# Delta-rule attention with a gated MLP: small products with 32-column stationaries in place of masked 64-column blocks

## The chip, the cores and the metric

The kernel runs on one core of one Trainium2 chip. The metric is device time in microseconds (us), from launch to the last output; lower is better. TensorE (PE) does the matrix products, its weight loads are shown as PEld; VectorE (DVE), ScalarE (ACT) and GpSimd (POOL) do elementwise work; SyncE (SP) issues most DMAs. A matmul loads a *stationary* operand (rows x columns) into the array and streams a *moving* operand through it.

## The reference

32 sequences (4 batches x 8 heads) of 768 tokens with head dimension 48 run a delta rule. All heads of a token are then joined to 384 channels, which pass through a gated MLP with 2048 hidden units.

```python
k_n = k / (np.linalg.norm(k, axis=-1, keepdims=True) + 1e-06)
for t in range(S):
    y[:, :, t] = np.einsum('bhd,bhde->bhe', q[:, :, t], state)
    v_old = np.einsum('bhde,bhd->bhe', state, kt)
    state = state + bt[:, :, :, None] * np.einsum('bhd,bhe->bhde', kt, vt - v_old)
...
h = x @ w_in
g = h - np.tanh(h)
return (g @ w_out).astype(np.float32)
```

## The kernel before, in words

**Tiling.** Time is cut into 24 chunks of 32 tokens (`C = 32`, `NS = 24`). A chunk holds 32 (batch, head) pairs of 32 x 32 (scores) or 32 x 48 (values). With 4 batches on the partitions, one chunk fills 128 partitions by 8 heads. Four chunks are a group (`NG = 6`), and four chunks are also one window of 512 tokens of the MLP (`W = 4`, six windows).

**One chunk.** `score` makes the key-key and key-query products. `solve(g)` inverts the 32 x 32 triangular systems of a whole group on DVE, a chain of some 60 dependent elementwise instructions that starts with a transpose (line 356) once all four chunks of the group are scored, and ends with another (line 438), which writes `tt`. `chain` then runs through the chunks one by one, since each needs the state that the one before left: keys times state (line 552), queries times state (570), subtraction from the values (`vsub`, 560), the inverted block times these (585), a copy to SBUF (`u_sb`, 591), two products that update the state (603), two by two additions into `st` (631), and the product of masked scores with the chunk values (614). `output` copies, transposes on PE (650) and splits the result into a high and a low part for the MLP.

**How two batches share a product.** A product covers two batches at a time. The stationary operand is a block matrix of 64 columns: keys or queries of two batches side by side (`kb`, `qb`, 112 rows, zero off the blocks), the inverted block doubled and masked (`tb`, lines 506), the scores doubled and masked (`pc`, 514). These blocks are built by copies: ACT copies keys and queries (lines 304 to 313, 526, 531), POOL builds `tb` and `pc` (DVE does it for the first four chunks), and ACT moves the scores out of PSUM (`pq`, 341).

**MLP.** For each window and each of 16 slices of 128 hidden units, nine matmuls with 512 moving columns make the hidden values (`ph`, line 722), `gate` works on them on ACT and DVE (733 to 742), and nine more accumulate the output (`po`, 765). Window 0 is done in two halves of 256 tokens. The weights arrive as 64-bit numbers in 32 pieces and are decoded on ACT and DVE (671 to 697) while window 0 runs.

**What sets the order.** `Plan` writes the order of every engine by hand, in advance: each step is an `Op` with an engine, an assumed cost, what it depends on and a rank. `run` picks the engine that can start first, and on it, among the steps that can start within `SLACK` (2.2 us on PE) of the earliest, the one with the smallest start less rank. Each engine then executes its list strictly in that order. PSUM has two banks `psa` for all small products, one `psy`, two `ph` and three `po`. `Ring` counts free buffers. Until a set time (46 us in the plan) PE's gaps are filled with dummy matmuls (`warm`, line 220).

## Time and profile before

| | us |
|---|---|
| median of 3 runs | 685.51 (680.96 to 686.44) |
| span of the profiled execution | 683.6 |
| PE busy | 634.8 |
| DVE busy | 424.5 |
| ACT busy | 294.6 |
| POOL busy | 77.9 |
| first MLP matmul starts | 69.4 |
| the second group's inverted blocks reach PE | 178.4 |
| first MLP matmul of window 1 starts | 220.4 |

The profiled execution's own time is known by its span, from the first to the last instruction; the runs' times take in the little that lies around it as well. Each fp32 product is executed as two passes, so 16 products stand as x32 in the rows. PE is busy for most of the span, but busy at two speeds: the row PEclk of the page gives the granted clock in tenths. Rows of a timeline give start, length, engine, line, operation, output and inputs, shape, count, and in brackets how long the engine had been idle and what ended that.

### The profile page before, as it was taken

The page shows a single profiled execution, that of the slowest core. Times are in us where ns is not written, and L with a number is a line of the kernel's source. Part 1 is how long each engine was busy: PE and PEld are TensorE (multiplying, and loading weights), DVE is VectorE, ACT ScalarE, POOL GpSimd, SP SyncE. Part 2 cuts the span into 40 slices and gives each one's busy share as a digit, 9 for nine tenths or more (in the row PEclk, how much of TensorE's full clock was granted, in tenths as well). Part 3 has the DMA queues.
Part 4 walks back from the last instruction along what each step waited for, and adds up shares of the span by engine and source line. Part 5 has one row for each costly group of instructions (what it writes and reads, how often), then busy time and mean ns, then how long its engine had stood idle before and what let it go on. Part 6 is the DMA issues. An engine that isn't in the chain of part 4 may idle for free.

```text
span 683.6 us, 18248 instructions
## 1 busy us (share of the span) xinstructions
PE 634.8 (93%) x7922; PEld 545.0 (80%) x7922; DVE 424.5 (62%) x982; ACT 294.6 (43%) x560; POOL 77.9 (11%) x81
## 2 busy tenths in 40 slices
PE   7697999899597998999989998999999999999996
PEld 4386999889596887888888887888878888888885
DVE  6975685898436884689737886388862434243242
ACT  4454369743354335642465235652342333233232
POOL 1000000100412004300133003310061000000000
PEclk9857589999558999999999999999999999999999
DMA  9439903000343004410153102430000010001001
GB/s 255 167 116 344 272 19 114 19 1 36 105 117 104 0 1 133 129 54 15 59 160 88 40 0 68 129 110 1 0 25 26 2 46 1 0 1 47 0 1 46
DMA packets 25056, 48.80 MB, mean 71 GB/s; under 512 B 3168, under 2 KB 15584, under 8 KB 24976
## 3 DMA queue, kind: packets, MB, share of 16 engines
q1 hardware_dynamic: 24832, 47.49, 22.9%
q8 instruction: 62, 1.02, 0.7%
q10 hardware_dynamic: 144, 0.15, 0.1%
q14 instruction: 18, 0.15, 0.1%
HBM read 42.91 MB, written 4.72 MB: 70 GB/s over the span
## 4 chain that ended last, share of the span: by engine, by line
PE 75%; issue 10%; ACT 6%; DVE 6%; DMA 2%; POOL 1%; SPq 0%; ACTq 0%; POOLq 0%; DVEq 0%
PE po L765 26%; PE ph L722 25%; PE psa L603 7%; PE psy L614 4%; PE psa L585 3%; PE psa L326 3%; PE psa L552 3%; PE psy L570 2%; ACT qb L531 1%; ACT kb L526 1%; PE psa L650 1%; DMA kd<-in_kq 1%; DVE st L631 1%; ACT u_sb L591 1%; ACT kb L313 1%
## 5 line engine op out<-in xcount | busy, mean ns | idle before, releaser
L722 PE MATMUL ph<-xt,w 128*128 128x512 f32 (+1 forms) x1008 | 211.8, 365 | 3.3 <-DVE t L735 2.7
L765 PE MATMUL po<-gh,w 128*128 128x512 f32 (+1 forms) x1008 | 211.8, 363 | 1.8 <-ACT gh L740 0.6
L722 PEld LDWEIGHTS ph<-xt,w 128*128 128x128 f32 x1008 | 173.8, 193 | 33.2 <-DVE t L735 3.7
L765 PEld LDWEIGHTS po<-gh,w 128*128 128x128 f32 x1008 | 171.2, 190 | 31.8 <-ACT gh L740 1.3
L733 ACT ACTIVATE t<-ph 128x512 f32<-128x512 f32 (+1 forms) x112 | 60.1, 537 | 153.9 <-PE ph L722 145.2
L735 DVE TENSOR_TENSOR t<-ph,t 128x512 f32<-128x512 f32 (+1 forms) x112 | 68.8, 615 | 80.1 <-ACT t L733 79.3
L740 ACT CAST gh<-t 128x512 fp32r<-128x512 f32 (+1 forms) x112 | 62.7, 559 | 86.2 <-PE po L765 40.8
L742 DVE TENSOR_TENSOR gh<-t,gh 128x512 fp32r<-128x512 f32 (+1 forms) x112 | 71.8, 642 | 43.6 <-ACT gh L740 41.5
L631 DVE TENSOR_TENSOR st<-st,psa 48x384 f32<-48x384 f32 x88 | 48.6, 552 | 62.9 <-PE psa L603 61.5
L603 PE MATMUL psa<-u_sb,kt 32*48 32x48 f32 x1472 | 49.2, 223 | 8.7 <-ACT u_sb L591 7.3
L603 PEld LDWEIGHTS psa<-u_sb,kt 32*48 32x48 f32 x1472 | 43.0, 136 | 15.1 <-ACT u_sb L591 9.7
L428 DVE TENSOR_TENSOR a<-a,tmp 128x30 f32<-128x30 f32 (+9 forms) x150 | 49.5, 330 | 4.1
L424 DVE TENSOR_TENSOR tmp<-a 128x30 f32<-128x30 f32 (+9 forms) x150 | 49.6, 331 | 3.7
L506 POOL TENSOR_TENSOR tb<-tt,cs 128x512 f32<-128x512 f32 x20 | 25.5, 1274 | 201.4 <-DVE tt L438 161.1
L585 PE MATMUL psa<-v,tb 64*64 64x48 f32 x768 | 31.6, 236 | 13.5 <-POOL tb L506 9.1
L585 PEld LDWEIGHTS psa<-v,tb 64*64 64x64 f32 x768 | 28.4, 150 | 15.6 <-POOL tb L506 9.3
L614 PE MATMUL psy<-u_sb,pc 64*64 64x48 f32 x768 | 31.9, 239 | 3.0 <-issue 2.2
L552 PEld LDWEIGHTS psa<-st,kb 112*64 112x64 f32 x736 | 27.3, 156 | 6.6 <-issue 3.1
L614 PEld LDWEIGHTS psy<-u_sb,pc 64*64 64x64 f32 x768 | 28.6, 153 | 4.8 <-issue 3.4
L552 PE MATMUL psa<-st,kb 112*64 112x48 f32 x736 | 29.6, 240 | 2.6 <-DVE st L631 2.4
L526 ACT COPY kb<-kd 48x512 f32<-48x512 f32 x44 | 27.1, 616 | 9.2 <-PE psa L552 8.7
L326 PE MATMUL psa<-kc,kb 112*64 112x64 f32 x704 | 29.8, 246 | 0.5 <-issue 0.3
(85 smaller groups left out, 521.6 us busy)
## 6 DMA issues: line engine op xcount, KB each, us to landing
kc<-in_kq SPq DMA_DIRECT2D x23, 448.0 KB, 4.1
kd<-in_kq SPq DMA_DIRECT2D x22, 448.0 KB, 4.0
raw<-in_w_in SPq DMA_DIRECT2D x16, 384.0 KB, 8.7
raw<-in_w_out SPq DMA_DIRECT2D x16, 384.0 KB, 8.2
v<-in_vn SPq DMA_DIRECT2D x24, 192.0 KB, 4.3
kt<-in_kn SPq DMA_DIRECT2D x24, 192.0 KB, 2.9
out<-o SPq DMA_DIRECT2D x18, 256.0 KB, 2.0
cs<-in_const ACTq DMA_DIRECT2D x1, 144.5 KB, 4.6
```

Of the source, the lines that this page charges most:

```text
L326: nc.tensor.matmul(ps[64 * pr:64 * pr + 64, h, :], cols(kb, u), kc[:, :, u, :], start=True, stop=True)
L552: nc.tensor.matmul(pk[64 * pr:64 * pr + 64, h, :], cols(kb, u), st[:, pr, h, :], start=True, stop=True)
L585: nc.tensor.matmul(pu[rows, h, :], tb[rows, h].rearrange("p b i -> p (b i)"), v[rows, h, :], start=True, stop=True)
L603: nc.tensor.matmul(ps[HALF[bp], h, :], kt[rows, h, :], u_sb[rows, h, :], start=True, stop=True)
L614: nc.tensor.matmul(py[rows, h, :], pc[rows, h].rearrange("p b i -> p (b i)"), u_sb[rows, h, :], start=(s == 0), stop=True, skip_group_chec ...
L631: nc.vector.tensor_tensor(st[rows, pr], st[rows, pr], ps[rows], ALU.add)
L722: nc.tensor.matmul(p, wi[f][:, a, ct, :], xt[:, b, ct, part], start=(ct == 0 and i == 0), stop=(ct == NC - 1 and i == 2))
L733: nc.scalar.activation(t_, p, AF.Tanh)
L735: nc.vector.tensor_tensor(t_, p, t_, ALU.subtract)
L740: nc.scalar.copy(gh[:, 0, :n], t_)
L742: nc.vector.tensor_tensor(gh[:, 1, :n], t_, gh[:, 0, :n].bitcast(F32), ALU.subtract)
L765: nc.tensor.matmul(po[c][:, part], wo[f][:, a, 128 * c:128 * c + 128], gh[:, b, :n], start=(f == 0 and i == 0 and z < 1), stop=(f == NF - ...
```

## The change

Each batch gets a product of its own, with a 32-column stationary, so that no block matrices have to be built. Where a block structure is still needed it moves to the *moving* operand, which may be wide.

- **Scores** (`products`): 32 products of 48 rows x 32 columns straight from the loaded keys, in place of 16 of 112 x 64 from copied ones. The first four chunks do keys first and queries later (`answers`), and load keys and queries as separate halves.
- **Masks**: DVE masks the scores as it takes them out of PSUM (`mask`, 256 elements). ACT's `pq` copy and POOL's `tb` and `pc` are gone, and so are all key and query copies with the tiles `kb` and `qb`.
- **Chain**: keys and queries times state are 16 products each with the loaded `kd` (112 x 32) and a block-diagonal state of 96 columns. The inverted block is used as it is, 32 products of 32 x 32. ACT spreads the chunk values with two scaled copies into a block-diagonal `ub`. The state update takes 16 products of 64 x 48 with 96 moving columns, in place of 32 of 32 x 48. The last product takes 32 of 32 x 32.
- **Loads**: a second host layout, `kp`, serves the scores and `kq` the chain; every chunk loads both.
- **Plan**: the order of chunk work changes. A PE step may carry a `hold` in place of the slack; chain steps after the first group hold PE for at most 0.2 us. Queries times state now stand after the inverted block, and the output product in a stream of its own. The dummy matmuls are issued in any gap until the first output unit of the MLP. Pool sizes change (`SOLS` 3 to 4, nine `pc`).

```diff
+    def products(ps, kc, x):
+        for u in range(16):
+            h, pr = divmod(u, 2)
+            for bp, rows in enumerate(HALF):
+                q = slice(64 * pr + 32 * bp, 64 * pr + 32 * bp + 32)
+                nc.tensor.matmul(ps[q, h, :], kc[rows, 0, u, :], kc[rows, x, u, :], start=True, stop=True)
+
+    def mask(s, ps, psr, scored):
+        (_, t) = yield Op("DVE", dve(256), (scored, const_in, rpc), 0.3)
+        pc = at.tile([128, H, C], F32, name="pc", bufs=PCS)
+        nc.vector.tensor_tensor(pc, ps[:, :, C:], strict, ALU.mult)
...
-            for bp, rows in enumerate(HALF):
-                nc.scalar.copy(kb[rows, :, bp, :], kc[rows, 0])
...
-        for u in range(16):
-            h, pr = divmod(u, 2)
-            nc.tensor.matmul(ps[64 * pr:64 * pr + 64, h, :], cols(kb, u), kc[:, :, u, :], start=True, stop=True)
...
-        hw.tensor_tensor(tb, tt[:, 8 * r:8 * r + 8, None, :].broadcast_to([128, H, 2, C]), blocks, ALU.mult)
...
-        hw.tensor_tensor(pc, pq[:, :, None, :].broadcast_to([128, H, 2, C]), strict, ALU.mult)
...
-            nc.scalar.copy(kb[rows, :, bp, :], kd[rows, 0])
...
-            nc.scalar.copy(qb[rows, :, bp, :], kd[rows, 1])
...
                 for u in range(16):
-                    h, pr = divmod(u, 2)
-                    nc.tensor.matmul(pk[64 * pr:64 * pr + 64, h, :], cols(kb, u), st[:, pr, h, :], start=True, stop=True)
...
+                    m, b = divmod(u, 4)
+                    nc.tensor.matmul(pk[32 * b:32 * b + 32, 2 * m:2 * m + 2, :], kd[:, 0, 4 * b + m, :], st[:, b, m],
+                                     start=True, stop=True)
...
+            for u in range(32):
+                h, b = divmod(u, 4)
+                rows = slice(32 * b, 32 * b + 32)
+                nc.tensor.matmul(pu[rows, h, :], tt[rows, 8 * r + h, :], v[rows, h, :], start=True, stop=True)
...
+                nc.scalar.activation(ub[:, :, 0], pu, AF.Copy, scale=odd[0])
...
+                nc.scalar.activation(ub[:, :, 1], pu, AF.Copy, scale=odd[1])
...
+                        nc.tensor.matmul(ps[HALF[h % 2], h // 2], kt[rows, h, :], ub[rows, h], start=True, stop=True)
...
+            nc.tensor.matmul(py[rows, h, :], pc[rows, h, :], ub[rows, h, b % 2, :],
+                             start=(s == 0), stop=True, skip_group_check=True)
...
+CHAIN_RANK, CHAIN_HOLD = 2.5, 0.2
...
-EXTRA = {0: ["v0"], 1: ["d1"], 3: ["v1"], 9: ["v2"], 13: ["k4"], 18: ["v3"], 24: ["b1"]}
+EXTRA = {0: ["q0"], 1: ["v0", "q1"], 2: ["q2", "d1"], 3: ["q3", "v1"], 7: ["d2"], 9: ["v2"], 13: ["k4"], 15: ["d3"], 18: ["v3"], 24: ["b1"]}
```

The order of the instructions shows what moved. On PE, in the third group of chunks, one chunk's steps stood close together before (`psa` and `psy` are PSUM tiles, `kb`/`qb` key and query blocks, `st` the state, `v` the values, `tb` and `pc` masked blocks, `u_sb` the chunk values, `kt` keys by token):

```order
L326 MATMUL psa<-kc_3539,kb_85 64x64 x16
L552 MATMUL psa<-st,kb_84 64x48 x16
L570 MATMUL psy<-st,qb_87 64x48 x16
L585 MATMUL psa<-v,tb 64x48 x16
L650 MATMUL psa<-cs,y_sb 128x128 x3
L603 MATMUL psa<-u_sb,kt 48x48 x16
L614 MATMUL psy<-u_sb,pc 64x48 x16
L603 MATMUL psa<-u_sb,kt 48x48 x16
```

Now, at the same place (`ub` are the spread chunk values; L746 and L701 are the MLP's output and hidden units):

```order
L303 MATMUL psa<-kc_3896 32x64 x32
L522 MATMUL psa<-st,kd_3493 32x96 x16
L746 MATMUL po_3626<-gh,w_1742 128x512 x3
L746 MATMUL po_3627<-gh,w_1742 128x512 x3
L746 MATMUL po_3628<-gh,w_1742 128x512 x3
L543 MATMUL psa<-v,tt_3835 32x48 x32
L565 MATMUL psy<-st,kd_3493 32x96 x16
L303 MATMUL psa<-kc_4003 32x64 x32
L629 MATMUL psa<-cs,y_sb 128x128 x3
L701 MATMUL ph<-xt_3177,w_1640 128x512 x9
L575 MATMUL psa<-ub,kt 48x96 x16
L593 MATMUL psy<-ub,pc 32x48 x32
```

An MLP unit now stands in each gap of a chunk's chain, also in the first chunks of a group, and the small products are 32 wide.

On ACT, while window 0 runs and the second group is scored (`gs` takes the key products, `t` and `gh` belong to the gate, `c` and `w` to the decoding of weights), these rows stood before:

```order
L313 COPY kb_85<-kc_1133 48x16x32 x2
L733 ACTIVATE t<-ph 128x256 x2
L740 CAST gh<-t 128x256 x2
L337 COPY gs_1229<-psa 128x8x32
L341 COPY pq<-psa 128x256
L733 ACTIVATE t<-ph 128x256
L526 COPY kb_83<-kd_1155 48x16x32 x2
L740 CAST gh<-t 128x256
L531 COPY qb_86<-kd_1155 48x16x32 x2
L733 ACTIVATE t<-ph 128x256
L526 COPY kb_84<-kd_1162 48x16x32 x2
L740 CAST gh<-t 128x256
```

And now:

```order
L347 COPY gs_1301<-psa 128x8x32
L674 CAST w_1853<-c_1768 128x384
L650 ACTIVATE c_1949<-raw_1442 128x384
L347 COPY gs_1301<-psa 128x8x32
L674 CAST w_1948<-c_1801 128x384
L712 ACTIVATE t<-ph 128x256
L650 ACTIVATE c_1985<-raw_1445 128x384
L719 CAST gh<-t 128x256
L712 ACTIVATE t<-ph 128x256
L674 CAST w_1967<-c_1834 128x384
L347 COPY gs_1301<-psa 128x8x32
```

The key copies are out of the row, and the second and third copies of `gs` stand closer together.

On SP, the first loads were these before:

```order
L227 DMA kc_94<-in_kq 112x1024
L227 DMA kc_100<-in_kq 112x1024
L227 DMA kd_103<-in_kq 112x1024
L227 DMA kd_109<-in_kq 112x1024
L246 DMA bt<-in_beta 128x32
L258 DMA raw_118<-in_w_in 128x3x256
```

And now:

```order
L230 DMA kc_91<-in_kp 112x512
L230 DMA kc_95<-in_kp 112x512
L230 DMA kd_99<-in_kp 112x512
L230 DMA kd_102<-in_kp 112x512
L249 DMA bt<-in_beta 128x32
L261 DMA raw_106<-in_w_in 128x3x256
L230 DMA kc_91<-in_kp 112x512
```

The first four key loads are half as large, and the query halves follow among the weights.

More of the change, by code (lines that the diff above doesn't have):

```diff
@@ L618, in chain @@
-            if s + 1 < NS:
-                state[s] = added[1]
-    def add(s, pr, ps, psr, e, added):
-        for n, rows in enumerate(HALF):
-            if s == 0 and pr:
-                (_, t) = yield Op("ACT", act(DM, True), (e, zero[5]), 2.5)
-                nc.scalar.copy(st[rows, pr], ps[rows])
-            else:
-                (_, t) = yield Op("DVE", dve(DM), (e, zero[5]), 1.5)
+                    m, b = divmod(u, 4)
+                    nc.tensor.matmul(py[32 * b:32 * b + 32, 2 * m:2 * m + 2, :], kd[:, 1, 4 * b + m, :], st[:, b, m],
+                                     start=(m == 0), stop=False, skip_group_check=True)
@@ L759, in out_units @@
             if w not in pos:
+                if not pos:
+                    plan.streams[:] = [x for x in plan.streams if x[0] is not idle]
                 pos[w] = ([ps_o.tile([128, T], F32, name=f"po{c}") for c in range(NC)], ro.take())
@@ L810, in preps @@
             yield from prep(s)
-    def keys():
-        for s in range(1, NS):
-            yield from prep_keys(s)
     def solves():
```

343 lines of the change are left out of this document (158 added, 185 removed).

## The prediction

> **What bounds the kernel now.** I read the page first, then the busy time by stage, then the chain of waits for what opens each stage, and last the timeline of PE in a few places. The page gives the span and the granted clock in 40 slices of 17.1 us:
>
> ```profile
> span 683.6 us, 18248 instructions
> PEclk9857589999558999999999999999999999999999
> ```
>
> The clock falls to about half in two places, in slices 2 to 4 (counted from 0) and in slices 10 and 11. The chain of waits shows what opens the stages (start, length, what): the transfer of the last key block, the transpose that starts a group's inversion, the first small product with state for chunks 1 to 3, the step that releases the second group, and the first MLP unit of window 1.
>
> ```profile
> 2.17 8.48 DMA kd<-in_kq
> ...
> 13.43 1.26 DVE a L356
> ...
> 45.50 1.95 PE psa L552 x32
> ...
> 55.13 1.14 PE psa L552 x32
> ...
> 72.34 1.88 PE psa L552 x32
> ...
> 118.58 1.25 DVE a L356
> ...
> 177.08 1.27 POOL tb L506
> 178.39 1.94 PE psa L585 x32
> ...
> 220.38 7.96 PE ph L722 x27
> ```
>
> I cut the run there. Each row is a stage: its length, then the busy time of PE, PEld, DVE, ACT and POOL, the granted clock, and DMA.
>
> ```profile
> 0.00:30.30 30.30, 22.61 (x250) 12.17 (x254) 23.50 (x96) 12.80 (x23) 3.49 (x11) 0.98 0.80 238
> 30.30:86.00 55.70, 48.02 (x1236) 44.63 (x1230) 37.37 (x80) 25.06 (x54) 0.00 (x0) 0.59 0.74 225
> 86.00:118.60 32.60, 31.58 (x311) 30.77 (x310) 21.25 (x52) 25.86 (x58) 0.00 (x0) 0.93 0.21 64
> 118.60:177.00 58.40, 48.29 (x451) 45.98 (x449) 52.31 (x150) 29.98 (x70) 2.18 (x3) 0.96 0.12 38
> 177.00:220.40 43.40, 38.48 (x813) 35.64 (x813) 18.30 (x44) 19.17 (x36) 14.45 (x14) 0.66 0.35 100
> 220.40:547.00 326.60, 314.55 (x4305) 267.94 (x4306) 226.49 (x500) 140.19 (x251) 57.76 (x53) 0.99 0.19 55
> 547.00:684.00 137.00, 131.29 (x577) 107.83 (x575) 45.27 (x67) 41.59 (x69) 0.00 (x0) 0.99 0.05 18
> ```
>
> So there are three regimes. Up to 177 the path runs through DVE: inversion, the first chunks, decoding, the second inversion (DVE busy 52.31 of 58.40 at the end). From 177 to 220.4 four chunks run one after another with nothing else to do, at a clock of 0.66. From 220.4 to 547 PE is the bound, 314.55 of 326.60; only the small products and the gaps can shrink there. The last 137 us are pure MLP, which the change leaves alone.
>
> **The price of small products.** In the third regime one chunk looks like this (start, length; the distance between starts is the price):
>
> ```profile
> 258.86 1.15 PE L326 MATMUL psa<-kc,kb 112*64 112x64 f32 x32
> 259.85 1.09 PE L552 MATMUL psa<-st,kb 112*64 112x48 f32 x32
> 260.76 1.10 PE L570 MATMUL psy<-st,qb 112*64 112x48 f32 x32
> 261.80 1.14 PE L585 MATMUL psa<-v,tb 64*64 64x48 f32 x32
> 262.86 1.15 PE L326 MATMUL psa<-kc,kb 112*64 112x64 f32 x32
> 265.18 0.92 PE L603 MATMUL psa<-u_sb,kt 32*48 32x48 f32 x32 [1.16 <-ACT u_sb L591]
> 266.03 1.14 PE L614 MATMUL psy<-u_sb,pc 64*64 64x48 f32 x32
> 267.09 0.92 PE L603 MATMUL psa<-u_sb,kt 32*48 32x48 f32 x32
> ```
>
> Scores 0.99, keys times state 0.91, queries 1.04, inverted block 1.06, update twice 0.85, scores times values 1.06: 6.76 us for 224 passes, 30.2 ns each. The only 32-column stationaries of this kernel (line 467) ran in a stretch at half clock:
>
> ```profile
> 38.47 1.10 PE L467 MATMUL psa<-tt,gs 32*32 32x16 f32 x64
> 39.50 1.52 PE L603 MATMUL psa<-u_sb,kt 32*48 32x48 f32 x32
> 40.95 1.95 PE L614 MATMUL psy<-u_sb,pc 64*64 64x48 f32 x32
> 42.82 1.51 PE L603 MATMUL psa<-u_sb,kt 32*48 32x48 f32 x32
> ```
>
> There 64 passes took 1.03 us (16 ns each), against 1.45 (39.50 to 40.95) for 32 passes with 48 columns (45 ns) and 1.87 (40.95 to 42.82) for 32 with 64 columns (58 ns). So narrow stationaries on separate quarters of the array go much faster per pass, even at half clock. At full clock the price is not shown; I bound it. *64 passes of 32 columns* (scores, inverted block, last product): 1.03 if the clock changes nothing, 0.59 if it scales as 1.87 to 1.06. I take 0.85, a little above the middle, since 48 or 64 columns move where line 467 moves 16. *Keys and queries times state* (32 passes of 32 columns, 96 moving in place of 48): at least half of 1.03, at most 0.91 doubled. Lines 326 and 552 differ by 16 moving columns and 0.08, so 48 more add 0.24 to 0.51: I take 0.75. *Update* (32 passes in place of 64, 96 columns moving): between 0.51 and 1.06, and 0.85 as for one group of line 603 now. A chunk without its scores then costs 4.05 against 5.77.
>
> The Trainium skill speaks against this ("TensorE: Matmul & The Clock Gate", section "Wait — 56ns, not 53.3ns?"): start-to-start of matmuls never drops below about 25 ns, however few columns move. By that an estimate for the 288 passes of a chunk is 7.2 us, above today's 6.76, and there would be no gain on PE. The trace disagrees, with 16 ns on line 467.
>
> **After 220.4.** 16 chunks save 1.72 each, 27.5; 12 scores save 0.14, 1.7. PE's gaps there are 12.05 us (326.60 less 314.55); with a hold of 0.2 us in place of 2.2 I take half of it back, 6. Against that stand more changes between large and small products:
>
> ```profile
> 293.28 2.34 PE L765 MATMUL po<-gh,w 128*128 128x512 f32 x9
> 295.55 0.92 PE L603 MATMUL psa<-u_sb,kt 32*48 32x48 f32 x32
> ...
> 300.77 6.28 PE L722 MATMUL ph<-xt,w 128*128 128x512 f32 x27
> ```
>
> A unit among small products takes 2.27, one among its like 2.09: 0.18. A group had four such places and now has nine or ten: 5.5 x 4 groups x 0.18 = 4. Net: 31.2 saved (ends: with every price at its low end and all gaps gone 66 saved, with every price at its high end and no gap won 20 lost).
>
> **Up to 177.** The other prices stand in the groups of instructions (busy, mean ns):
>
> ```profile
> L631 DVE TENSOR_TENSOR st<-st,psa 48x384 f32<-48x384 f32 x88 | 48.6, 552 | 62.9 <-PE psa L603 61.5
> L313 ACT COPY kb<-kc 48x512 f32<-48x512 f32 x40 | 24.7, 616 | 1.0 <-DMA kc<-in_kq 0.4
> L560 DVE TENSOR_TENSOR v<-v,psa 128x384 f32<-128x384 f32 x23 | 12.7, 550 | 15.9 <-PE psa L552 15.2 <-POOL a L377 0.5
> L591 ACT COPY u_sb<-psa 128x384 f32<-128x384 f32 x24 | 11.5, 480 | 19.4 <-PE psa L585 18.9
> L514 DVE TENSOR_TENSOR pc<-pq,cs 128x512 f32<-128x512 f32 x4 | 2.7, 684 | 0.0
> L334 DVE TENSOR_TENSOR gs<-psa,cs 128x256 f32<-128x256 f32 x4 | 2.4, 599 | 0.8 <-PE psa L326 0.7
> 10.73 0.62 ACT L304 COPY qb<-kd 48x512 f32<-48x512 f32 x1 [0.20 <-DMA kd<-in_kq]
> ```
>
> *Opening.* The last of four key blocks lands at 10.73, the inversion starts at 13.43. Its transfer holds the chain for 8.48; four loads of half the size take half of that, 4.2 less, and the 0.62 copy goes. I take 3.5, since DVE puts three masks near the inversion (ends 0 and 5). The query halves come behind the first weights and wait for nothing on the path.
> *DVE's work* from 30.3 to 177 is 37.37 + 21.25 + 52.31 = 110.9, so 35.8 idle. Eight block builds of 0.684 go (5.5), seven masks of at most 0.60 come (4.2): 109.6.
> *DVE's idle time.* From 86 to 118.6 it is 11.35, while ACT is 25.86 of 32.60 busy, with 14 key copies of 0.616, 8.6 in all, that delay gates and scores. They are gone; I take 8 back. From 30.3 to 86 it is 18.33, with the clock at 0.59 and chunks 9.6 and 17.2 us apart (45.50, 55.13, 72.34). A chunk now needs 0.75 + 0.55 + 0.85 + 2 x 0.48 (two spreading copies) + 0.85 + 4 x 0.552 = 6.2, with some 0.1 for each of six hand-overs 6.8; dummy matmuls keep the clock up until the first output unit. I take 13 back. DMA is no cover here: SP still stands at an early load (now `d2`, which needs chunk 1 done; before `v2`, which needed chunk 0), so weights come no sooner. The 6.1 of the last stretch stay. Idle left: 14.7.
> The second inversion so ends at 30.3 - 3.5 + 109.6 + 14.7 = 151.1: 25.9 saved (ends: 4.8 with no idle time won, 34).
>
> **From 177 to 220.4.** Between 178.39 and 220.38, 42 us. Four chunks of 6.8 are 27.2, the first shortened by its keys, the last lengthened by output and transposes, 30 in all; the clock may fall again, since the dummy matmuls have ended, which adds up to 1 us a chunk: 33. 9 saved (ends 0 and 14). POOL's 1.27 ahead of it is within this.
>
> **At nothing** I cost the mask on DVE after 220.4 (16 x 0.60 = 9.6, in 100 us of idle DVE: 326.60 less 226.49), the second spreading copy there (MLP units fill PE), and the loads for two more chunks' keys (DMA share 0.19).
>
> **Sum.** 683.6 - 25.9 - 9 - 31.2 = 617.5. The median of the runs, 685.51, lies 1.9 above the profiled span; I keep that: 619.
>
> **Rivals.**
> *A, a pass costs the same whatever its width.* For it: 45 to 58 ns at half clock but 27 to 33 at full clock, so widths differ less when fast. Against: 16 ns on line 467. At 30.2 ns, 288 passes are 8.69, 1.93 more per chunk: 16 x 1.93 + 4 = 34.9 lost, no gain in the second regime, 4.8 in the first: 683.6 + 30.1 + 1.9 = 716, slower. It decides above 6.76 / 288 = 23.5 ns per pass. By the 25 ns of the Trainium skill's page on TensorE, named above, the same estimate gives 0.44 more per chunk and 693 us; that is a case inside this rival.
> *B, the second inversion ends no sooner*, because decoding, loads or the fixed order hold DVE as before. For it: DVE is already 90% busy in the last 58 us. Against: 29.7 idle before. Then 4.8 remain of 25.9: 640.
> *C, DVE becomes late after 220.4*, because its load goes from 226 of 327 to 236 of 295 us and PE waits for an inverted block at each group. At 4 us for four groups: 635.
>
> **Numbers.** The forecast 0.60, B 0.20, C 0.12, A 0.05, better than all my terms 0.03. The range 592 to 655 takes in B, C and half of the spread of the pass prices. One per cent is about what a measurement of this kernel can tell from no change. Only A ends above it; a pass price near the turning point with nothing won before 177 would give no change. Faster 0.92, same 0.03, slower 0.05.
>
> **What would show it.** Right: 64-pass groups (scores, inverted block, last product) 0.6 to 1.0 us apart from the next start, keys times state near 0.75; the second transpose of line 356's kind near 95 us rather than 118.58 and the first MLP unit of window 1 near 185; no key copies on ACT; PE's gaps after that under 8 us. Wrong: passes above 23 ns, a window 1 that starts after 205, or PE waiting on DVE's inverse or masks in each group.

## The result and the profile after

| | before | after |
|---|---|---|
| median of the runs, us | 685.98 (4 runs) | 647.17 (4 runs, 645.46 to 650.57) |
| ratio, 95% interval | | 0.950 (0.942 to 0.957) |
| span of the profiled execution | 683.6 | 648.8 |
| PE busy | 634.8 | 596.1 |
| first MLP matmul of window 1 starts | 220.38 | 212.18 |
| from there to the end | 463.2 | 436.6 |

The kernel is faster by 38.8 us in the medians, inside the range of 592 to 655, and well short of the 66 that were forecast. Medians here and below are of all executions, while the ratios leave out disturbed ones, to which the profiled execution of the kernel before with the short hold belongs, so that no profile of that run is used. The head of the page of the changed kernel, with the queue that brings instructions (packets, MB, share of 16 DMA engines):

```profile
span 648.8 us, 21619 instructions
PEclk9966899899767899999999999999999999999999
q8 instruction: 76, 1.25, 0.8%
```

And that queue on the page of before:

```profile
q8 instruction: 62, 1.02, 0.7%
```

There are 3371 more instructions, and 0.23 MB more of them to fetch. Below, the changed kernel in stages like those of before (length, busy PE, PEld, DVE, ACT, POOL, clock, DMA share):

```profile
0.00:31.00 31.00, 22.58 (x504) 12.35 (x505) 18.85 (x88) 3.69 (x6) 2.35 (x9) 1.00 0.66 181
31.00:86.00 55.00, 44.71 (x1432) 37.48 (x1431) 37.55 (x87) 26.43 (x62) 0.00 (x0) 0.75 0.60 193
86.00:111.00 25.00, 23.96 (x418) 22.96 (x417) 22.79 (x55) 17.30 (x40) 0.00 (x0) 1.00 0.76 209
111.00:170.00 59.00, 50.55 (x514) 48.12 (x514) 50.09 (x141) 21.06 (x52) 3.17 (x4) 0.93 0.12 37
170.00:212.20 42.20, 31.37 (x1069) 25.15 (x1069) 22.67 (x59) 9.82 (x19) 3.85 (x5) 0.70 0.42 117
212.20:648.80 436.60, 422.95 (x5808) 340.20 (x5808) 269.11 (x568) 139.90 (x246) 16.61 (x21) 0.99 0.17 49
```

The last stage of before, in one row for comparison:

```profile
220.40:683.60 463.20, 445.84 (x4880) 375.76 (x4880) 271.76 (x566) 181.77 (x320) 57.76 (x53) 0.99 0.15 44
```

There is the gain, 26.6 of 34.8. The stretch between the second inverse and that stage is about as long as it was (42.2 against 43.4). The early part lost its idle DVE time only behind 86 us (2.21 of 25.00 idle, where it was 11.35 of 32.60); from 31 to 86 DVE still idles 17.45. The second inversion starts at 108.58, where it started at 118.58:

```profile
108.58 1.24 DVE L362 STREAM_TRANSPOSE a<-gs 128x1024 f32<-128x1024 f32 x1
```

The view of DVE's waits from 31 to 86 adds up to 10.2 us for PE and 6.6 for ACT, and has none that ends in a load. The largest (us in total, times, longest) are those for the *joins* (lines 473 and 485), small products that put the first group's inverted blocks together from halves, and for the decoding of weights on ACT:

```profile
DVE tt L488 <- PE psa L485: 6.0, 3, 3.3
DVE w L676 <- ACT w L674: 2.6, 3, 1.3
```

On PE, the timeline shows the new prices in the last regime (the distance between starts is the price):

```profile
244.99 1.10 PE L303 MATMUL psa<-kc 48*32 48x64 f32 x64
246.02 0.87 PE L522 MATMUL psa<-st,kd 112*32 112x96 f32 x32
246.81 2.34 PE L746 MATMUL po<-gh,w 128*128 128x512 f32 x9
249.08 0.88 PE L543 MATMUL psa<-v,tt 32*32 32x48 f32 x64
249.89 0.87 PE L565 MATMUL psy<-st,kd 112*32 112x96 f32 x32
250.69 0.52 PE L303 MATMUL psa<-kc 48*32 48x64 f32 x21
...
267.23 0.88 PE L575 MATMUL psa<-ub,kt 64*48 64x96 f32 x32
268.04 0.88 PE L593 MATMUL psy<-ub,pc 32*32 32x48 f32 x64
268.85 1.45 PE L701 MATMUL ph<-xt,w 128*128 128x512 f32 x5
```

Scores take 1.03, every other group 0.79 to 0.81, the unit 2.27. A chunk is 5.05 (1.03 + 0.79 + 0.81 + 0.80 + 0.81 + 0.81) where it was 6.76, for 288 passes in place of 224: 17.5 ns a pass, and 12.7 where 64 passes move 48 columns.

**A new stop.** The opening, on PE's timeline, shows what the forecast had not thought of. The fourth score stops in its middle, waiting for no engine (`issue`):

```profile
6.55 1.50 PE L303 MATMUL psa<-kd 48*32 48x32 f32 x89
12.98 0.71 PE L303 MATMUL psa<-kd 48*32 48x32 f32 x36 [4.93 <-issue]
13.46 0.24 PE L303 MATMUL psa<-kc 48*32 48x32 f32 x1
13.48 0.26 PE L303 MATMUL psa<-kd 48*32 48x32 f32 x3
13.51 1.08 PE L303 MATMUL psa<-kc 48*32 48x32 f32 x63
14.53 1.04 PE L215 MATMUL po<-wz 128*128 128x512 bf16 x2
15.49 0.54 PE L303 MATMUL psa<-kc 48*32 48x32 f32 x22
16.82 0.80 PE L303 MATMUL psa<-kc 48*32 48x32 f32 x42 [0.79 <-issue]
```

Between the two stops stand 36 + 1 + 3 + 63 + 2 + 22 = 127 matmuls. With a weight load each that is 254 instructions, and 1.25 MB in 76 packets is 16.4 KB a packet, or 256 instructions if one takes 64 bytes: PE stops where a packet of its program ends. The trace has the times of these packets as well. In the stop of 4.93 the next packet begins to move at 10.46 and lands at 11.59, and PE goes on at 12.98. All 13 such stops of this trace end 1.3 to 1.6 us after a packet of that queue has landed, and 2.4 to 2.8 after it began to move: what PE waits for is its program. What the DMA engines did in that stop and in a later one:

```profile
8.00:13.00 5.00, 0.07 (x9) 0.02 (x3) 0.62 (x2) 1.10 (x2) 0.00 (x0) 1.00 1.10 291
59.90:62.60 2.70, 0.00 (x0) 0.00 (x0) 0.42 (x2) 0.78 (x2) 0.00 (x0) 0.50 1.07 269
```

They were full of data (shares of 1.10 and 1.07). The later one falls into a join, as does one before it, and chunk 2's keys times state start behind them at 63.53, 18.8 us after those of chunk 1 (44.70):

```profile
56.34 0.83 PE L485 MATMUL psa<-yj,tn 16*32 16x16 f32 x47 [1.87 <-issue]
...
62.67 0.93 PE L485 MATMUL psa<-yj,tn 16*32 16x16 f32 x51 [2.83 <-issue]
63.53 1.51 PE L522 MATMUL psa<-st,kd 112*32 112x96 f32 x32
```

The view of waits, all PE waits ending in `issue` added, gives 16.1 us of such stops over the span, where before had 8.5. I call this *theory I*: the program comes over the same DMA engines as the data, narrow products need more of it, and a packet that is late stops PE. *Theory W* holds the late weights responsible instead: SP, which issues all loads, stands at the loads of the twin keys `d1`, `d2`, `d3`, which wait for a buffer (`kd`, two of them):

```profile
27.08 0.48 SPq L259 DMA_DIRECT2D raw<-in_w_out  x1
49.88 0.33 SPq L222 DMA_DIRECT2D kd<-in_kq  x1
...
57.48 0.41 SPq L259 DMA_DIRECT2D raw<-in_w_out  x1
69.93 0.33 SPq L222 DMA_DIRECT2D kd<-in_kq  x1
```

SP does nothing from 27.6 to 49.9 and from 57.9 to 69.9. *Theory O* asks how much is owed to the order of the steps and the shorter `hold`, and not to the products.

### The profile page after: what moved, and what is told of

Read it like the earlier page. It is cut to its first block, busy times and chain, and to the rows that moved or that the text cites. A ratio compares the mean times of both kernels' runs of the same rounds, so it can differ in the third digit from the quotient of the medians.

```text
span 648.8 us, 21619 instructions
## 1 busy us (share of the span) xinstructions
PE 596.1 (92%) x9742; PEld 486.3 (75%) x9742; DVE 421.1 (65%) x991; ACT 218.2 (34%) x424; POOL 26.0 (4%) x39
## 3 DMA queue, kind: packets, MB, share of 16 engines
q8 instruction: 76, 1.25, 0.8%
## 4 chain that ended last, share of the span: by engine, by line
PE 85%; DVE 6%; issue 4%; DMA 3%; ACT 2%; ACTq 0%; DVEq 0%
PE ph L701 31%; PE po L746 30%; PE psa L303 4%; PE psa L543 4%; PE psa L575 3%; PE psy L565 3%; PE psa L522 3%; PE psy L593 3%; PE po L215 2%; PE psa L629 2%; DMA kc<-in_kp 2%; DMA raw<-in_w_in 1%; PE psa L473 1%; DVE a L434 1%; DVE st L610 1%
## 5 line engine op out<-in xcount | busy, mean ns | idle before, releaser
L746 PE MATMUL po<-gh,w 128*128 128x512 f32 (+1 forms) x1008 | 215.1, 365 | 2.8 <-ACT gh L719 1.9
L701 PE MATMUL ph<-xt,w 128*128 128x512 f32 (+1 forms) x1008 | 215.0, 367 | 1.8 <-DVE t L714 1.1
L701 PEld LDWEIGHTS ph<-xt,w 128*128 128x128 f32 x1008 | 172.7, 192 | 32.9 <-DVE t L714 1.8
L746 PEld LDWEIGHTS po<-gh,w 128*128 128x128 f32 x1008 | 170.4, 190 | 33.6 <-ACT gh L719 2.3
L543 PEld LDWEIGHTS psa<-v,tt 32*32 32x32 f32 x1536 | 21.3, 118 | 20.3 <-DVE v L529 12.6
L303 PE MATMUL psa<-kc 48*32 48x64 f32 (+1 forms) x1536 | 29.4, 229 | 6.8 <-issue 3.3
L543 PE MATMUL psa<-v,tt 32*32 32x48 f32 x1536 | 25.1, 220 | 11.2 <-DVE v L529 9.5
L303 PEld LDWEIGHTS psa<-kc 48*32 48x32 f32 x1536 | 24.9, 119 | 13.0 <-issue 6.8
L501 POOL TENSOR_TENSOR v<-v,nt 128x384 f32<-128x384 f32 x20 | 16.5, 829 | 274.6 <-DMA v<-in_vn 200.1
L650 ACT ACTIVATE c<-raw 128x384 f32<-128x384 f32 x32 | 17.3, 554 | 29.4 <-DMA raw<-in_w_out 12.6
L575 PE MATMUL psa<-ub,kt 64*48 64x96 f32 x736 | 24.4, 269 | 2.8 <-DVE pc L308 0.8
L575 PEld LDWEIGHTS psa<-ub,kt 64*48 64x48 f32 x736 | 18.4, 132 | 10.7 <-issue 6.4
L635 DVE TENSOR_TENSOR xt<-psa,xt 128x384 fp32r<-128x384 f32 x24 | 13.3, 556 | 19.6 <-ACT xt L633 19.3
L522 PE MATMUL psa<-st,kd 112*32 112x96 f32 x736 | 23.2, 273 | 2.7 <-PE psa L629 1.3
```

The source lines that it names most:

```text
L303: nc.tensor.matmul(ps[q, h, :], kc[rows, 0, u, :], kc[rows, x, u, :], start=True, stop=True)
L543: nc.tensor.matmul(pu[rows, h, :], tt[rows, 8 * r + h, :], v[rows, h, :], start=True, stop=True)
L575: nc.tensor.matmul(ps[HALF[h % 2], h // 2], kt[rows, h, :], ub[rows, h], start=True, stop=True)
L701: nc.tensor.matmul(p, wi[f][:, a, ct, :], xt[:, b, ct, part], start=(ct == 0 and i == 0), stop=(ct == NC - 1 and i == 2))
L746: nc.tensor.matmul(po[c][:, part], wo[f][:, a, 128 * c:128 * c + 128], gh[:, b, :n], start=(f == 0 and i == 0 and z < 1), stop=(f == NF - ...
```

## The experiments

All are edits of the changed kernel unless said. "Stops" are the waits for instructions of the profiled execution, over its whole span; "first unit" is the first MLP matmul of window 1, and the next column runs from there to the end. Each ratio is against the kernel before, measured beside the run. The stages are those of one execution each, and the changed kernel's profiled one was the slowest of its four (650.57, where the fastest took 645.46), so that differences of a few us between single stages can be chance.

| run | median us | ratio (95%) | stops | first unit | rest |
|---|---|---|---|---|---|
| before | 685.98 | | 8.5 | 220.4 | 463.2 |
| after | 647.17 | 0.950 (0.942 to 0.957) | 16.1 | 212.2 | 436.6 |
| three `kd` buffers | 661.63 | 0.967 (0.957 to 0.977) | 32.0 | 225.4 | 434.7 |
| keys ahead | 656.73 | 0.961 (0.953 to 0.969) | 23.5 | 219.8 | 435.6 |
| dummies between windows | 649.23 | 0.950 (0.942 to 0.958) | 17.8 | 208.3 | 438.8 |
| hold 2.2 | 682.96 | 0.999 (0.994 to 1.003) | 29.5 | 206.2 | 474.1 |
| quiet opening | 648.25 | 0.946 (0.937 to 0.956) | 15.0 | 208.0 | 436.9 |
| before, hold 0.2 | 671.76 | 0.979 (0.967 to 0.990) | - | - | - |
| three `kd`, paced weights | 657.85 | 0.962 (0.954 to 0.970) | 15.9 | 221.0 | 435.0 |
| update in 32 products | 660.49 | 0.967 (0.958 to 0.976) | 25.9 | 218.6 | 445.7 |
| queries before, hold 2.2 | 669.24 | 0.975 (0.969 to 0.980) | 34.7 | 223.5 | 444.8 |
| opening and fill | 648.27 | 0.944 (0.939 to 0.949) | 17.8 | 203.4 | 443.0 |
| queries before, hold 0.2 | 665.49 | 0.973 (0.966 to 0.980) | 33.3 | 217.5 | 447.2 |
| opening, no fill | 647.54 | 0.946 (0.940 to 0.951) | 17.2 | 203.6 | 440.9 |

### A third buffer for the twin keys

```diff
-    rkc = {"kc": Ring(2), "kd": Ring(2)}
+    rkc = {"kc": Ring(2), "kd": Ring(3)}
```

(and `bufs=3` for the `kd` tiles).

> The changed kernel with a third buffer for the chain's keys (tile kd), so that the loads d2 and d3 no longer hold up the weights behind them on SP; nothing else differs. Theory W (late weights cost the first stage what the prediction gave it): the last weights are issued near 70 us in place of 87, the second inversion starts 8 to 14 us sooner than 111, window 1 starts 8 to 14 us sooner than 212.8, and the time falls by 8 to 12 us. Rival P (PE's own stops, in the opening and before chunk 2, set the pace): weights come sooner, but the time stays within 3 us.

Measured: 661.63, 14 us slower than the changed kernel, which is in neither expectation. The weights did come sooner, the last one issued at 72.6 to 75.0 in place of 84.7 to 87.1. But the stops in the first 100 us rose from 11.5 to 27.0. Two of them, with the DMA share in the column before the last:

```profile
15.70:21.40 5.70, 0.01 (x2) 0.00 (x0) 5.19 (x28) 1.10 (x2) 0.73 (x4) 0.50 1.06 276
...
62.20:66.70 4.50, 0.01 (x2) 0.01 (x2) 0.00 (x0) 0.05 (x1) 0.00 (x0) 0.50 1.07 339
```

In the second nothing runs at all: DVE's list is in a fixed order too, and stands at a result of PE. DVE was busy 28.40 us from 31 to 86, against 37.55, and the second inversion started at 121.16. So theory W is right that SP stands, but freeing SP did not help. The reading that fits the stops is that its stand had kept the DMA engines free for PE's program (DMA share from 31 to 86: 0.60 in the changed kernel, 0.72 here). One thing more differs: the plan now puts chunks 2 and 3 ahead of the first MLP unit (97.1 in place of 65.0), so the stops need not be the whole of the loss.

### The first keys and queries ahead of the weights

```diff
-LOADS = ["k0", "k1", "k2", "k3", "b0"]
+LOADS = ["k0", "k1", "k2", "k3", "b0", "q0", "q1", "q2", "d1"]
```

> The changed kernel with the order of the first loads changed: query halves 0 to 2 and the first chain keys go ahead of the first weights, so that little else is in transfer while the first scores run. Theory F (PE stands for 4.93 us in the middle of the fourth score because its own instructions arrive late behind data transfers): the stop falls below 1 us, the first inversion starts at 10 to 11 us in place of 14.41, and the time falls by 2 to 4 us. Rival (the stop is a wait for the key block or for a PSUM bank): it stays at 4 to 5 us.

Measured: 656.73, slower by 9.6. The stop in the fourth score stayed, at 3.83, nearer to the rival than to theory F; the stages just ahead of it and in it are

```profile
4.60:8.00 3.40, 2.89 (x218) 2.58 (x218) 1.81 (x3) 0.00 (x0) 0.00 (x0) 1.00 1.06 243
8.00:11.70 3.70, 0.00 (x0) 0.00 (x0) 0.00 (x0) 0.00 (x0) 0.00 (x0) 0.63 0.21 49
```

The DMA engines were full beside the scores and mostly idle in the stop itself. The packet began to move at 9.18, when they had nearly emptied, and PE went on at 11.73. So a full queue delays the packet, and a part of the stop is left when the queue has emptied. All stops of the first 100 us together came to 17.6, where the changed kernel has 11.5.

### Dummies between window 0 and window 1

Dummy matmuls also fill the gaps between the last unit of window 0 and the first of window 1, where the clock had fallen.

```diff
+    def warm_between():
+        while 1 not in begun:
+            yield Op("PE", 0.22, (rh, lambda: 0.0 if len(ended) else None), rank=-9.0, mode="warm", hold=0.0)
...
+            nc.tensor.matmul(ph.rearrange("p (a b) -> p a b", a=4), wz, wide, start=True, stop=True)
```

> The changed kernel with dummy matmuls also in PE's gaps between the end of window 0 and the first unit of window 1 (into free ph banks). Theory C (the half clock makes each group of small products 1.44 us instead of 0.81 there): the clock of that stretch goes from 0.70 to above 0.95, the stretch from the second group's release to the first unit of window 1 shrinks from 42 to 32 to 34 us, and the time falls by 7 to 10 us. Rival H (hand-overs between PE, ACT and DVE set the pace of the chunks): the clock rises, but the stretch loses less than 3 us.

Measured: 649.23, the same. The first unit came 3.9 sooner, the rest took 2.2 longer. From the second inverse to the first unit the row is

```profile
169.80:208.30 38.50, 32.53 (x1133) 21.18 (x1121) 23.61 (x61) 10.15 (x20) 3.87 (x5) 1.00 0.49 138
```

The clock is full, and the stretch is only 3.1 shorter than the 41.6 of the changed kernel: close to rival H, and far from theory C.

### The hold as before

```diff
-CHAIN_RANK, CHAIN_HOLD = 2.5, 0.2
+CHAIN_RANK, CHAIN_HOLD = 2.5, 2.2
```

> The changed kernel with the planner's hold for chain steps put back from 0.2 to 2.2 us. Theory N (after window 1 starts, the gain comes from the narrower and fewer passes, and the order only fills gaps): PE's gaps from there to the last chunk rise from 8 to 12 to 16 us, and the time rises by 2 to 8 us. Rival O (the order carries most of the 27 us): the time rises by 15 us or more.

Measured: 682.96, the whole gain gone, as rival O has it. In the groups of instructions the inverted blocks' row (busy, mean ns, idle before) says where:

```profile
L543 PE MATMUL psa<-v,tt 32*32 32x48 f32 x1536 | 26.5, 223 | 28.7 <-DVE v L529 23.1 <-issue 3.6 <-DVE pc L308 1.3
```

PE stands 23.1 us for `v`, because the changed order puts the inverted blocks right behind the keys' products. The stops grow as well, from 2.8 to 12.7 between 220 and 460: groups that stand back to back use up 128 matmuls in 1.6 us (two groups of 64 at 0.81), and that is less than the 2.4 to 2.8 us from the start of a packet's transfer until PE goes on.

### A quiet opening

The first weight load, and all behind it on SP, waits for the fourth score (a one-column copy from its mask into the weight's buffer makes the load wait).

```diff
+            elif item == "w0":
+                deps = (gram_done[0][3],)
...
+        if i == 0:
+            nc.gpsimd.tensor_copy(raw[:, 0:1], groups[0][0][:, 0, 24:25])
```

> The changed kernel, but the first weight load (and with it everything behind it on SP's queue) waits until the fourth score is masked, so that no data moves while PE runs the four scores. Theory I (PE's stops inside a group of products are late instructions, which come over the same DMA engines as the data: in the changed kernel's profile the DMA share was 1.10 in the stop of 4.93 us at 8.0 to 13.0): the stop in the fourth score falls below 1 us, the inversion starts at about 9.5 to 10.5 in place of 14.4, the joins at 29.5 to 30.5 in place of 34.1, and the span is 3 to 5 us shorter (about 645). Rival S (a stop of fixed length when a block of instructions runs out, whatever the DMA engines do): the stop stays at 4 to 5 us, and the span is the same within 1 us. Rival W (the end of the second inversion hangs on when the weights come, not on the first): the stop goes, and the span is the same or 1 to 3 us longer, since the weights start later.

Measured: the stop fell from 4.93 to 1.31, its packet began to move at 6.52 in place of 10.46, and the inversion started at 10.60 in place of 14.41. The stage of the stop, with no data under way:

```profile
8.00:9.20 1.20, 0.05 (x5) 0.05 (x7) 0.13 (x1) 0.00 (x0) 0.00 (x0) 1.00 0.00 0
```

That supports theory I for most of the stop, and shows a remainder of 1.3 us that is there without any load. But the joins (`tt`) won only 1.2 of the 3.8 us. On DVE's timeline, the inverse is there at 27.4:

```profile
26.38 1.03 DVE L455 STREAM_TRANSPOSE tn<-a 128x512 f32<-128x512 f32 x1
```

On PE's, the joins (line 477 here) stand behind dummies (line 215) that the plan had counted out for a later inverse:

```profile
23.17 9.81 PE L215 MATMUL po<-wz 128*128 128x512 bf16 x39
32.92 2.00 PE L477 MATMUL psa<-tt,gs 32*32 32x16 f32 x128
```

The median did not change (648.25), as rival W of this run said, while the profiled span, 644.9, is the 645 of theory I: the time does not decide between them. The second inversion started at 113.83, later than in the changed kernel.

### Before, with the short hold

The kernel before, its chain's steps with a hold of 0.2 from chunk 4 on.

```diff
-            rank = 4.0 if s < 4 else CH
+            rank, hold = (4.0, 2.2) if s < 4 else (CH, 0.2)
```

> The kernel before with one thing of the change: the chain's steps of chunks 4 and later may hold back other PE work for 0.2 us in place of 2.2. All products, copies and the order inside a chunk are those of before. Theory P (the shorter product groups carry the gain after 220.4: small products took 201 us of PE before and 153 after): between 675 and 690, with the stretch from the third inversion's start to the end within 6 us of before's 462.8. Rival O (the hold carries it: the changed kernel lost 33 us when its hold went back to 2.2): 650 to 668.

Measured: 671.76, between the two expectations. The hold by itself is worth 2.1% (1.0 to 3.3), some 14 us, where the whole change is worth 5.0%, and it has nothing to do with narrow products.

### Three buffers, with paced weights

```diff
+            elif kind == "w" and n >= PACE:
+                deps = ((lambda n=n: turned[n - PACE][1].t if n - PACE in turned else None),)
...
+        if i >= PACE:
+            nc.gpsimd.tensor_copy(raw[:, 0:1], turned[i - PACE][0][:, 0:1].bitcast(I32))
...
+PACE = 2
```

> The run with three key buffers (660.1 us span, PE's stops for instructions 27.0 us in its first 100 us), with one thing more: the load of weight piece i waits until piece i-2 has been converted, so that at most two pieces are under way at once. Theory I: the DMA engines are no longer full without a break, the stops in the first 100 us fall to 15 us or less, and the span is 645 to 652. Rival W (what cost the time there was the order of the plan, with the joins of chunks 2 and 3 ahead of the first MLP unit): 656 or more, even if the stops shrink. If the pacing itself is too slow, the last weight is issued later than 90 and the span is over 660.

Measured: the stops in the first 100 us fell from 27.0 to 12.6, as theory I says. The time was 657.85 all the same, which is rival W's. The pace was slow, with the last weight issued at 107.6 and later (84.7 to 87.1 in the changed kernel), so the run shows that fewer loads under way mean fewer stops, and not what that would be worth with the weights on time.

### The update in 32 products

```diff
-                    for p, rows in enumerate(PAIR):
...
-                        nc.tensor.matmul(ps[HALF[h % 2], h // 2], kt[rows, h, :], ub[rows, h], start=True, stop=True)
+                    for q in range(4):
+                        rows = slice(32 * q, 32 * q + 32)
...
+                        nc.tensor.matmul(ps[HALF[q % 2], h // 2, h % 2], kt[rows, h, :], ub[rows, h, q % 2], start=True, stop=True)
```

> The changed kernel with the update's 16 products of 64 rows by 96 columns a chunk made 32 products of 32 rows by 48 columns, interleaved over the four groups of 32 rows (64 passes in place of 32). The state is then laid out in another order than its readers take it, so the outputs are not the reference's. Theory C (a group's time follows the moving columns that each quarter of the array takes: 64x48 over four, as the inverted blocks' 0.81): the group stays at 0.8 to 0.9, and the span is within 3 us of 648.8, a little of it more stops for instructions. Rival M (each pass costs about 25 ns whatever its shape, as the update's 32 passes in 0.81 and before's 64 in 1.70): 1.6 to 1.7 a group, and the span is 664 to 672.

Measured, on PE's timeline:

```profile
276.39 0.93 PE L576 MATMUL psa<-ub,kt 32*48 32x48 f32 x64
277.25 0.88 PE L594 MATMUL psy<-ub,pc 32*32 32x48 f32 x64
```

64 passes in 0.86 us, 13.4 ns each: theory C is right on the price. Before, the same 64 passes took 1.70, in two groups that each used only two groups of 32 rows. What made the update cheap is that all four are at work, not that there are fewer passes. Yet the time was 660.49, far from theory C's, though not for rival M's reason: the extra passes cost 0.05 each chunk, but there are 6 more packets (82), and stops of 25.9 us in place of 16.1. These 9.8 are less than the 13.3 that the median grew by; the remainder stays open.

### Queries before the inverted blocks, with either hold

The products of the change in the order of before: queries times state between keys times state and the inverted blocks; first with the hold of 2.2, then with 0.2.

```diff
                 plan.spawn(vsub())
+                (_, t) = yield small(0.75, (ry,))
+                py, pyr = bank("psy")
...
             else:
                 sub = get(s, "v", 2)
...
-            if s > 0:
-                (_, t) = yield small(0.75, (ry,))
-                py, pyr = bank("psy")
```

> The changed kernel's products with the order and the hold of before: the queries' products stand again between the keys' and the inverted blocks', and a step of chunk 4 or later may hold other PE work back for 2.2 us. It is put beside the two runs that moved one of them each: the changed kernel with the hold of 2.2 (682.96, nothing left of the gain) and the kernel before with the hold of 0.2 (671.76). Theory P (shorter groups carry the gain, and the hold of 2.2 only hurt because the changed order puts the inverted blocks right behind the keys' products, where PE stood 23.1 us for v): 655 to 665, with less than 5 us of waits for v. Rival O (products and order gain little while the chain holds PE): 674 to 685. Rival I (groups back to back outrun PE's instructions, 12.7 us of such stops between 220 and 460 in the run with the hold of 2.2): the waits for v go, but stops for instructions of 10 us or more stay there, and the time lies between, 665 to 674.

Measured: 669.24, which is rival I's range. Between 220 and 460 PE waits 1.0 us for `v`, where it waited 11.2 in the run with the changed order and the hold of 2.2; the stops there, 8.9, are a little under the 10 of rival I. From the first unit on, the row of the stages is

```profile
223.80:668.30 444.50, 419.44 (x5808) 341.84 (x5807) 269.21 (x571) 140.40 (x246) 15.71 (x20) 1.00 0.16 48
```

PE busy is 419, even less than in the changed kernel (423). But it is idle 25.1 where the changed kernel idles 13.7, and 6.1 of that difference are stops (8.9 against 2.8).

> The run with the changed kernel's products and the queries' products put back ahead of the inverted blocks (669.24), with one thing more: the hold of 0.2 in place of 2.2. It fills the last corner of products, order and hold. If the hold is worth the same with both sorts of products (14.8 with the old ones: 686.5 to 671.76), the time is 652 to 657, and the changed order is worth 5 to 10 of the gain. Rival: with the short hold PE does other work while VectorE subtracts, so that the order inside a chunk no longer matters, and the time is 645 to 650.

Measured: 665.49, slower than both expectations. The short hold gained only 3.8 here; the order is worth 18.3 us with it, and costs 13.7 without it (669.24 to 682.96). The stops are 17.2 more (33.3 less 16.1), but they do not match the time stage by stage: in the first 100 us they are 10.2 more, and the first unit comes 5.3 later; between 220 and 460 they are 6.7 more, and the rest takes 10.6 longer. So the stops go with the loss, and how much of it they make is not shown.

### Two versions meant to be faster

Both have the quiet opening, 44 dummies ahead of the joins in place of 70, and `d1` behind `v1`; the first has the dummies between the windows too.

```diff
-EXTRA = {0: ["q0"], 1: ["v0", "q1"], 2: ["q2", "d1"], 3: ["q3", "v1"], 7: ["d2"], 9: ["v2"], 13: ["k4"], 15: ["d3"], 18: ["v3"], 24: ["b1"]}
+EXTRA = {0: ["q0"], 1: ["v0", "q1"], 2: ["q2"], 3: ["q3", "v1", "d1"], 7: ["d2"], 9: ["v2"], 13: ["k4"], 15: ["d3"], 18: ["v3"], 24: ["b1"]}
...
-            yield Op("PE", 0.22, rank=-9.0, mode="warm", hold=0.0)
+            yield Op("PE", 0.22 if plan.free["PE"] < 20.0 else WARM, rank=-9.0, mode="warm", hold=0.0)
...
+WARM = 0.4
```

> A version meant to beat the changed kernel (647.17): its products and order, with (1) no load beside the first four scores, as in the run with the quiet opening (fourth score's stop 4.93 to 1.31, inversion 14.4 to 10.6); (2) fewer dummy products before the joins, 44 in place of 60 to 70, since there the joins stood behind dummies until 32.92 while the inverted blocks were ready at 27.4; (3) the load of chunk 1's twin keys behind chunk 1's values, so that SP doesn't stand before them (DVE waited 3.91 us for values there); (4) dummies between window 0's last unit and window 1's first. Theory I and the plan's dummies (the first joins are what the early stages hang on): joins at 27.5 to 29.5, the second inversion 3 to 5 us sooner than after's (131.0 on VectorE), time 638 to 643. Rival W (VectorE's decode of the weights, which come no sooner, sets when the second inversion starts): joins sooner, second inversion within 1.5 us of 131, time 645 to 648. Rival F (earlier weight loads meet the joins, whose 512 products need eight blocks of instructions): stops of 15 us or more in the first 100 us, time 650 or more.

> The version meant to beat the changed kernel without the dummies between window 0 and window 1; there the first unit of window 1 came at 203.6 (after: 212.5), but from there to the end it took 442.8 (after: 436.3). Theory: the opening's part of that (joins at 30.2 in place of 34.1, second inversion 4.8 sooner) holds by itself, the stretch with half a clock costs 4 to 5 again, and from the first unit on it goes as in the changed kernel: first unit at 207 to 209, span 643 to 646. Rival: the later stretch gives back whatever the early one wins, with fill or without: first unit at 209 or before, span 647 or more.

Measured: 648.27 and 647.54, no different from the changed kernel. The early part improved as meant: joins at 30.2 and 30.0, first unit 8.6 to 8.8 sooner. With the fill, the step that the expectation puts at 131 (a step within the second inversion, which starts at 108.58) came at 126.25, so theory I held there; the time is close to rival W's. Without the fill the profiled span, 644.5, is in the theory's range, but the medians show no gain over the changed kernel. The rest gave back 4.3 to 6.4 of the early gain, 2.4 of that as stops (5.2 against 2.8); what the remainder is, or whether it is chance between single executions, stays open. The fill of the first did keep the clock up where three chunks follow one another between the windows:

```profile
180.10:203.40 23.30, 20.41 (x704) 13.28 (x704) 18.65 (x51) 6.09 (x13) 3.87 (x5) 1.00 0.41 115
```

The same three chunks without the fill:

```profile
177.70:203.60 25.90, 19.03 (x688) 15.10 (x685) 18.24 (x49) 7.12 (x14) 3.84 (x5) 0.82 0.40 113
```

That is 7.8 us a chunk at full clock and 8.6 at 0.82: the chain of hand-overs sets most of the length there, and not the clock.

## Why the prediction was right and wrong

**The last regime: right, 26.6 against 31.2.** A chunk without its scores costs 4.02 (forecast 4.05): keys, queries and update came out at 0.79 to 0.81 (forecast 0.75, 0.75, 0.85), the 64-pass groups at 0.81 (0.85). Scores went to 1.03, not down to 0.85, which costs 12 x 0.18 = 2.2. PE busy fell by 22.9 there. The gaps shrank by 3.7 (17.36, which is 463.20 less 445.84, to 13.65) where I had taken 6, and 2.8 of what is left are stops between 220 and 460. Rival A fell with the pass prices: 17.5 ns a pass, below the turning point of 23.5. The floor of 25 ns that I cited from the Trainium skill's "TensorE: Matmul & The Clock Gate" does not hold for products on separate quarters of the array (12.7 ns). The same page of the Trainium skill says in "Part 3: Packing small matmuls — row/col tiling" that tiles run concurrently in one array; the trace agrees, with 64 passes in 0.81 here, and 0.86 against 1.70 in the update.

**Up to the second inverse: wrong, 6.5 against 25.9.** The second inverse is ready at 170.5 (before 177.0, forecast 151.1). Four terms made up the forecast:

- *DVE idle from 86 on, 8 to win back*: right, 9.1 came back.
- *DVE idle from 30 to 86, 13 of 18.33 to win back*: this is the step that failed. It is 17.45 still. I had put a chunk at 6.8 us, its own steps with 0.1 for each hand-over, and nothing between chunks. Chunks 1 and 2 start 18.8 us apart (9.6 before): the joins stand between them, and the two stops in the joins, 1.87 and 2.83, pass on to DVE, whose two longest waits (1.91 and 3.31) are for these joins. The dummies did not keep the clock up either: it was 0.75 from 31 to 86, and the inverted blocks of chunk 1 took 1.43 (46.88 to 48.31) in place of 0.81. No wait of DVE there ends in a load, so the trace does not put the idle time down to late weights, although SP stands at `d1` to `d3` (the plan, which reckons with the time of each load, may have put other work around them). When SP does not stand (three buffers), the stops are longer, and DVE is idle longer. In no run did the second inversion start before 107.7, so no edit of the loads brought it forward by as much as 1 us; what the stage would take without the stops was not run.
- *Opening, 3.5*: it started 1.0 later (14.41 against 13.43). The half-size loads did bring the first score forward by 2 us (4.60 against 6.60); the stop of 4.93 ate that. With the quiet opening it starts at 10.60, 2.8 sooner than before, close to the forecast.
- *The last stretch, 6.1 idle to stay*: 8.9 of 59.00 (111 to 170). The inversion itself took 62.0 us (from 108.58 to its end) in place of 58.4, which gives back 3.5 of the 10 by which it started sooner.

Rival B (no sooner second inverse, 640) was close to what happened, 647. The forecast itself missed by 28 us; the time lies in the range because the range took in rival B, and that is luck as far as my terms go. Of the signs that I had named, the prices came out (scores, at 1.03, just over the 1.0), but the second inversion started at 108.58 and not near 95, and window 1 at 212.18, past the 205 that was to show me wrong. Two sums in the text are slightly off without touching the forecast: 1.03 scaled as 1.87 to 1.06 is 0.58, and the case of 25 ns inside rival A comes to 692 by that rival's own sum.

**From 177 to 220: wrong, 1.8 against 9.** From the inverse to the first unit of window 1 it takes 41.6 (before 43.4). I took 33, with up to 1 us a chunk for the clock; the clock did fall (0.70), but kept at 1.00 a chunk still takes 7.8, not 6.8: the sum of its steps was too small. Rival C (DVE late after 220) did not come: from 212.2 on PE waits 0.8 us for DVE in all.

**What the change's own parts brought.** All of the change but the moved queries and the hold gains 2.5% (686 to 669). The hold alone gains 2.1% on the old kernel. Together, in the old order, they gain 2.7%, so they do not add up. The moved queries bring the remaining 18 us, and only with the short hold; moved queries with the old products were not run. My forecast had the hold as half of 12 us of gaps and the order as nothing: its sum after 220 was near the mark, but not for the reasons given to each part, and so partly by luck. That narrower products use more program, and that the order decides when PE uses it up, was in none of the rivals.

## What to carry to other kernels

Spread small products over all four quarters of the array: the time went by the moving columns that each quarter takes (0.79 to 0.81 us for 64 passes of 48 columns or 32 of 96, 1.03 for 64 of 64), and not by the number of passes. But count the instructions that this adds, and keep them from standing back to back or beside full DMA queues, since PE's program comes through the same engines. Before late loads are held responsible for an engine's idle time, read in its own waits what ended them. Before freeing a queue that stands, ask what it was keeping free; and test an order and its hold together, since each alone can lose what both gain.

## What the hardware showed that was not expected

- PE takes its program in packets of 16.4 KB, 128 matmuls with their weight loads. It stops at the end of a packet if the next is late: over all runs 0.2 to 2.2 us where the DMA engines were idle ahead of the packet, and up to 6.2 us where they were full. The Trainium skill describes such blocks of 16 KiB ("Runtime: NRT & Kernel Launch", section "Instruction fetch mechanics") and calls the cost mostly hidden. The trace agrees on the block, and not on the cost: 16.1 us of 648.8 here, 34.7 of 668.3 in the worst run.
- More stops mostly went with more time, but the time is not their sum. Against the profiled span of the changed kernel (648.8): three buffers 15.9 more stops and 11.3 longer, keys ahead 7.4 and 6.6, queries before with the short hold 17.2 and 15.9; but the paced weights 7.2 longer with no more stops, and the hold of 2.2 longer by 31.5 with 13.4 more.
